# Some 32x128 products of a cross network's matmul stream split into four on 32x32 tiles

## The chip, the cores and the metric

The kernel runs on one core of one Trainium2 chip. The metric is the device time of one execution in microseconds (us). Before the change it is 467.46 us, the median of two runs (467.14 to 467.78). The span of a profile is the time from the first to the last instruction of one profiled execution.

## The reference

A cross network of six layers on a batch of 16384 rows with 416 columns, all in bf16:

```python
x = x0
for l in range(6):
    proj = jnp.einsum('bd,de->be', x, ws[l]) + bs[l]
    x = x0 * proj + x
```

`x0` is 16384 x 416, `ws` is 6 x 416 x 416, `bs` is 6 x 416.

## The kernel before

**Tiling.** The batch is cut into 8 groups `g` of 2048 rows. The activations lie transposed: features on the partitions, batch rows along the free axis. A layer's 416 features are three full tiles of 128 (`t` or `i` = 0, 1, 2) and a tail of 32. A group and a layer together are a job `(g, l)`. A job's output tile `i` has four chunks `j` of 512 batch rows, and one chunk fills one of the 8 banks of PSUM. The four tails of a group, 32 features each, share one tensor of 128 partitions, one quarter for each chunk; `quad` says which quarter a chunk has.

**A chunk's products.** The sum over 416 features is cut into 13 products of 32 features. Each is a matmul with 32 rows of the array (one row group `r` = 0 to 3) and 128 columns. The profile writes it 32\*128: 32 x 128 weights, 32 x 512 moving values, into 128 partitions of one bank. Twelve come from the full tiles (line 1040: three for each row group), the thirteenth from the tail (line 1044). Products of the four row groups can run beside each other in the array; those of one row group follow each other. At any time the four row groups work on different chunks, in different banks, and a chunk passes from one row group to the next.

**Other shapes.** The tail outputs are computed in `tails` as 128x32 tiles (line 697: 128 features into 32 partitions, four column groups beside each other), with corners of 32x32 tiles (line 685). At the beginning and the end of the kernel there are also full 128x128 matmuls (line 650), column quarters (line 638) and row and column quarters (line 665, in `rows32`, when `small` is set).

**After the products.** ScalarE reads a finished bank and adds the bias (line 550, in `evacuate_chunk`). VectorE multiplies two chunks at a time by `x0` (line 562) and adds `x` (line 567). The result is the next layer's input. With that reading the bank is free again.

**What sets the order.** Most of the kernel is one call of `stream`. Its order is written out by hand: the string `ORDER` gives for each step the row group and the chunk, with a `|` where a batch of tails stands. `replay` turns it into a list of single products with planned times (in its own units, a product takes `SLOT` = 20), sorts them by time, and hands out banks. `stream` walks that list (`plan`) and records each product in order; an entry with `r < 0` is a batch of tails. There are 6504 such products. TensorE executes in the order in which they are recorded. `Program` adds semaphore waits where an operation needs another engine's result, or a bank that another row group has written: two products on TensorE in the same row group need no wait, those of different row groups in the same bank do (the argument `row`).

The few lines that matter for the tile of a product are these:

```python
kw = dict(start=count[c] == 1, stop=count[c] == 4 * NT + 1, tile_position=(r * T32, 0))
```

## Time and profile before

| | |
|---|---|
| median of the runs | 467.46 us |
| span of the profiled execution | 465.7 us |
| mean granted TensorE clock | 0.997 |
| matmuls recorded / weight loads recorded | 7827 / 7833 |
| stream: first L1040 to the last | 40.7 to 429.1 us |
| L697 (tails, 128x32) | 33.6 us busy, x564 |
| L685 (corners, 32x32) | 7.1 us busy, x188 |
| L665 (quarters, 32x32) | 0.9 us busy, x32 |

PE is TensorE's matmuls, PEld its weight loads, DVE VectorE, ACT ScalarE, SP the queue that issues most DMAs. Each matmul has its own weight load ahead of it. Busy time is the time in which at least one instruction of the group is open, so matmuls that overlap are counted once; the mean duration of a matmul is its latency. L1040 is line 1040 of the kernel before. In the time-ordered view a line is a merged group: start in us, length in us, engine, line, operation, operands, count.

### The profile page before, as it was taken

How to read it: one execution, taken by the hardware profiler on the slowest of the kernel's cores; microseconds unless marked ns; L12 is line 12 of the kernel's file. 1: busy time of each engine (PE TensorE's matmuls, PEld its weight loads, DVE VectorE, ACT ScalarE, POOL GpSimd, SP SyncE). 2: the span in 40 equal slices, each digit the busy share in tenths (PEclk: the TensorE clock that was granted, in tenths of full speed). 3: DMA queues.
4: the chain of work that ended last, by engine and by line, in shares of the span. 5: the costliest groups of instructions: out<-in, count | busy, mean ns of one | idle time of the engine just before them, and what ended most of it. 6: DMA issues, size and time to landing. Idle time of an engine off the chain costs nothing.

```text
span 465.7 us, 17469 instructions
## 1 busy us (share of the span) xinstructions
PE 458.9 (99%) x7827; PEld 263.8 (57%) x7833; DVE 404.2 (87%) x700; ACT 379.1 (81%) x608; POOL 6.8 (1%) x15
## 2 busy tenths in 40 slices
PE   9999999999999999999999999999999999999995
PEld 5444566555556677555655556565575566755442
DVE  2887998989989899979989898888989889898897
ACT  4687888788888888888878888788887887889785
POOL 1000000000000000000000000000000000000000
PEclk9999999999999999999999999999999999999998
DMA  8986949101002978084858437990100095027899
GB/s 229 185 177 144 160 113 190 29 3 26 1 4 38 158 210 155 22 141 149 149 92 154 145 78 141 160 296 23 25 2 4 25 148 172 14 49 169 183 161 292
DMA packets 139087, 53.77 MB, mean 115 GB/s; under 512 B 112762, under 2 KB 138500, under 8 KB 139012
## 3 DMA queue, kind: packets, MB, share of 16 engines
q1 hardware_dynamic: 138856, 52.54, 52.5%
q8 instruction: 61, 1.00, 0.9%
q10 hardware_dynamic: 156, 0.11, 0.1%
q14 instruction: 14, 0.11, 0.1%
HBM read 5.97 MB, written 13.63 MB: 42 GB/s over the span
## 4 chain that ended last, share of the span: by engine, by line
PE 93%; DVE 4%; DMA 1%; issue 1%; ACT 0%; SPq 0%; DVEq 0%
PE ps L1040 70%; PE ps L697 7%; PE ps L1044 6%; PE ps L650 6%; PE ps L638 2%; PE ps L685 1%; DMA wm<-in_ws_dram 1%; DVE x L1194 1%; DVE x L1188 1%; DVE x L528 1%; DVE tw L523 1%; PE ps L671 1%; ACT tw L514 0%; PE ps L789 0%; SPq L734 0%
## 5 line engine op out<-in xcount | busy, mean ns | idle before, releaser
L1040 PE MATMUL ps<-x,wm 32*128 32x512 bf16 x6000 | 356.0, 374 | 0.0
L550 ACT ACTIVATE tw<-ps,bias 128x512 bf16<-128x512 f32 x500 | 310.5, 688 | 46.4 <-PE ps L1040 35.9
L1040 PEld LDWEIGHTS ps<-x,wm 32*128 32x128 bf16 x6000 | 212.5, 92 | 127.7 <-ACT tw L550 4.1
L562 DVE TENSOR_TENSOR tw<-tw,x 128x1024 bf16<-128x1024 bf16 x250 | 168.2, 689 | 39.6 <-ACT tw L550 38.9
L567 DVE TENSOR_TENSOR x<-tw,x 128x1024 bf16<-128x1024 bf16 x250 | 163.5, 690 | 0.3
L1044 PE MATMUL ps<-x,w 32*128 32x512 bf16 x504 | 151.7, 374 | 0.0
L1044 PEld LDWEIGHTS ps<-x,w 32*128 32x128 bf16 x504 | 42.7, 92 | 6.6
L514 ACT ACTIVATE tw<-ps,bias 128x512 bf16<-128x512 f32 (+1 forms) x46 | 35.0, 839 | 12.0 <-PE ps L671 7.9
L650 PE MATMUL ps<-x,wm 128*128 128x512 bf16 x146 | 33.6, 379 | 1.0 <-issue 0.8
L697 PE MATMUL ps<-x,wm 128*32 128x512 bf16 x564 | 33.6, 380 | 0.0
L608 ACT ACTIVATE ts<-ps,bias 128x512 bf16<-128x512 f32 x33 | 21.0, 687 | 14.7 <-PE ps L685 14.7
L523 DVE TENSOR_TENSOR tw<-tw,x 128x1024 bf16<-128x1024 bf16 (+1 forms) x35 | 21.4, 627 | 4.9 <-ACT tw L514 4.7
L650 PEld LDWEIGHTS ps<-x,wm 128*128 128x128 bf16 x152 | 13.9, 98 | 19.0 <-issue 3.2
L697 PEld LDWEIGHTS ps<-x,wm 128*32 128x32 bf16 x564 | 13.5, 96 | 18.7 <-ACT tw L550 4.7
L528 DVE TENSOR_TENSOR x<-tw,x 128x1024 bf16<-128x1024 bf16 (+1 forms) x35 | 20.6, 624 | 0.0
L612 DVE TENSOR_TENSOR x<-ts,x 128x512 bf16<-128x512 bf16 x47 | 18.4, 420 | 0.4
L610 DVE TENSOR_TENSOR ts<-ts,x 128x512 bf16<-128x512 bf16 x33 | 13.0, 418 | 0.0
L604 DVE SCALAR_TENSOR_TENSOR ts<-ps,bias,x 128x512 bf16<-128x512 f32 x14 | 10.5, 748 | 2.2 <-PE ps L685 2.2
L909 POOL COPY ost<-ot 128x512 bf16<-128x512 bf16 x6 | 5.3, 890 | 411.3 <-DMA ot<-x 411.3
L1130 PE MATMUL ps<-wm,x 128*128 128x416 bf16 x48 | 9.8, 340 | 0.1
L1182 ACT ACTIVATE x<-ps 128x416 bf16<-128x416 f32 x16 | 7.6, 518 | 2.4 <-PE ps L1130 2.4
L799 DVE COPY x<-ps 128x512 bf16<-128x512 bf16 x5 | 2.0, 423 | 8.5 <-PE ps L789 8.5
(50 smaller groups left out, 76.9 us busy)
## 6 DMA issues: line engine op xcount, KB each, us to landing
out_dram<-ost SPq DMA_DIRECT2D x6, 1664.0 KB, 7.1
x<-x SPq DMA_DIRECT2D x24, 96.0 KB, 2.3
x<-in_x_dram SPq DMA_DIRECT2D x8, 208.0 KB, 4.4
x<-in_x_dram SPq DMA_DIRECT2D x4, 416.0 KB, 8.0
out_dram<-ost SPq DMA_DIRECT2D x2, 832.0 KB, 6.0
wm<-in_ws_dram SPq DMA_DIRECT2D x5, 312.0 KB, 3.4
x<-x SPq DMA_DIRECT2D x22, 64.0 KB, 2.0
out_dram<-x SPq DMA_DIRECT2D x3, 416.0 KB, 4.8
```

Source lines behind the costliest of these rows:

```text
L514: add("act", lambda h, a=a, w=w, b0=b0: h.activation(tw[r][:, a * CH:(a + w) * CH], psum[:, b0 * CH:(b0 + w) * CH], ACT_F.Identity, bias=b ...
L523: add("dve", lambda h, a=a, e=e: h.tensor_tensor(tw[r][:, a * CH:e * CH], tw[r][:, a * CH:e * CH], x0s[s0][:, i * GC + a * CH:i * GC + e * ...
L528: add("dve", lambda h, a=a, e=e: h.tensor_tensor(xs[so][:, i * GC + a * CH:i * GC + e * CH], tw[r][:, a * CH:e * CH], src(i, a, e), ALU.ad ...
L550: add("act", lambda h: h.activation(tw[r][:, j * CH:(j + 1) * CH], bank(b), ACT_F.Identity, bias=bias[:, i, l:l + 1], scale=1.0), reads=[( ...
L562: add("dve", lambda h: h.tensor_tensor(tw[r][:, o], tw[r][:, o], x0s[s0][:, c], ALU.mult), reads=[("tw", r, k) for k in both] + [x0_tok(s0 ...
L567: add("dve", lambda h: h.tensor_tensor(xs[so][:, c], tw[r][:, o], src(i, a, a + 2), ALU.add), reads=[("tw", r, k) for k in both] + [stok(i ...
L608: add("act", lambda h: h.activation(ts[r][:, :], bank(b), ACT_F.Identity, bias=bias[:, 3, l:l + 1], scale=1.0), reads=[("ps", b), "bias"], ...
L612: add("dve", lambda h: h.tensor_tensor(x3s[so][:, :], ts[r][:, :], res, ALU.add), reads=[("ts", r)] + rtok, writes=[("x3", so), ("x3", so, ...
L650: add("pe", lambda h, t=t, j=j, k=k, w=w: h.matmul(bank(banks[j])[:, k * w:(k + 1) * w], wm[l][:, t, ecols], src(t, j, j + 1)[:, k * w:(k ...
L697: add("pe", lambda h, t=t, j=j, src=src, l=l, b=b, ro=ro, qo=qo: h.matmul(psum[qo, b * CH:(b + 1) * CH], wm[l][:, t, NT * P:D], src(t, j, ...
L1040: add("pe", lambda h, l=l, t=t, j=j, b=b, q=q, ecols=ecols, src=src, kw=kw: h.matmul(bank(b), wm[l][q, t, ecols], src(t, j, j + 1)[q, :], ...
L1044: add("pe", lambda h, l=l, b=b, q=q, ecols=ecols, s3=s3, kw=kw: h.matmul(bank(b), w3[l][q, ecols], s3[q, :], **kw), reads=tok3 + [("w3", l ...
```

## The change

Four stretches of the stream are picked by the number of tails batches that came before in the stream (`at_run`) and the product's place since the last batch (`in_run`, counted from 0). A picked product of 32 rows by 128 columns is issued as four of 32 rows by 32 columns, with the same moving values, into the four quarters of the same bank:

```diff
+        quarters = [0, 0]
         for _, r, c, b in plan:
             if r < 0:
                 ...
                 tails(due.pop(0)[1], corners_last=True, banks=c)
+                quarters[:] = [quarters[0] + 1, 0]
                 continue
             ...
+            at_run, in_run = quarters[0], quarters[1]
+            quarters[1] += 1
+            if {3: 100 <= in_run < 164, 5: 100 <= in_run < 164 and in_run % 8 == 0,
+                    7: 100 <= in_run < 164 and r == 0, 9: 100 <= in_run < 116}.get(at_run, False):
+                for m in range(4):
+                    o = slice(m * T32, (m + 1) * T32)
+                    km = dict(kw, tile_position=(r * T32, m * T32))
+                    wcols = slice(i * P + m * T32, i * P + (m + 1) * T32)
+                    if t < (NT if c < len(chunks) - keep else part):
+                        lhs, rhs, got = wm[l][q, t, wcols], src(t, j, j + 1)[q, :], [stok(t, j), wm_tok(l, i)]
+                    else:
+                        lhs, rhs, got = w3[l][q, wcols], s3[q, :], tok3 + [("w3", l, r)]
+                    add("pe", lambda h, b=b, o=o, lhs=lhs, rhs=rhs, km=km: h.matmul(
+                        psum[o, b * CH:(b + 1) * CH], lhs, rhs, **km),
+                        reads=got, writes=[("ps", b)], row=r)
+                if count[c] == 4 * NT + 1:
+                    evacuate_chunk(g, l, i, j, b, read[c])
+                continue
```

In the stream as built this picks 64 products one after another, 8 single ones (each eighth, all of row group 3), 16 single ones (row group 0's, each fourth) and 16 one after another. They are the stream's products 1189 to 1252, 2117 to 2173, 3050 to 3110 and 3880 to 3895. In the profile before they begin at 112.9, 168.1, 223.9 and 273.8 us. Every other instruction is as before. In the changed file the lines after the insertion are 20 further down: line 1040 becomes 1060, line 1044 becomes 1064, and the quarters are recorded at line 1053.

## The prediction

> **What bounds the kernel now.** I read the page from the top: busy shares, the 40 slices, the chain of waits; then the costliest groups, the time-ordered view around every change of tile shape, and the starts of single matmul records, which the trace keeps to the nanosecond (the view rounds to 10 ns).

> ```profile
> PE 458.9 (99%) x7827; PEld 263.8 (57%) x7833; DVE 404.2 (87%) x700; ACT 379.1 (81%) x608; POOL 6.8 (1%) x15
> PEclk9999999999999999999999999999999999999998
> PE 93%; DVE 4%; DMA 1%; issue 1%; ACT 0%; SPq 0%; DVEq 0%
> L1040 PE MATMUL ps<-x,wm 32*128 32x512 bf16 x6000 | 356.0, 374 | 0.0
> L550 ACT ACTIVATE tw<-ps,bias 128x512 bf16<-128x512 f32 x500 | 310.5, 688 | 46.4 <-PE ps L1040 35.9
> ```

> TensorE carries 93% of the chain and is never idle ahead of the stream's products (0.0 idle at L1040). ScalarE waits for TensorE (35.9 us), not the other way. So what TensorE loses inside the stream moves the end one for one. What it could absorb is small: only at 203.96 us does it lose more than 0.1 us to ScalarE or VectorE in the stretch concerned (the four row groups restart 68 to 260 ns late, mean 0.20 us).

> A product's 374 ns is its latency, not its pace. In the first stretch that the change touches:

> ```profile
> 114.64 0.37 PE L1044 MATMUL ps<-x,w 32*128 32x512 bf16 x1
> 114.80 0.42 PE L1040 MATMUL ps<-x,wm 32*128 32x512 bf16 x4
> 115.02 0.38 PE L1044 MATMUL ps<-x,w 32*128 32x512 bf16 x2
> 115.04 0.57 PE L1040 MATMUL ps<-x,wm 32*128 32x512 bf16 x4
> 115.26 0.37 PE L1044 MATMUL ps<-x,w 32*128 32x512 bf16 x1
> 115.28 0.56 PE L1040 MATMUL ps<-x,wm 32*128 32x512 bf16 x4
> 115.50 0.37 PE L1044 MATMUL ps<-x,w 32*128 32x512 bf16 x1
> ```

> From 114.64 to 115.50 there are 1+4+2+4+1+4 = 16 products in 0.864 us: each row group starts one every 216 ns, four groups beside each other, so 54 ns a product. A reader should take this round of 216 ns as the unit.

> Now the changes of tile shape that the kernel already makes:

> ```profile
> 85.86 0.60 PE L697 MATMUL ps<-x,wm 128*32 128x512 bf16 x8
> 86.40 0.42 PE L685 MATMUL ps<-x,w 32*32 32x512 bf16 x12
> 86.75 0.82 PE L1040 MATMUL ps<-x,wm 32*128 32x512 bf16 x10
> ```

> The last L697 starts 309 ns before the first L685; the last L685 starts 317 ns before the first L1040. In place of 216 ns a shape change costs a start-to-start of 304 to 318 ns everywhere in the stream. The way back from 32x32 to 32x128 is shown 14 times, always 317 or 318 ns after the last corner product of all. The first L1040 is always of row group 0, while that group's own last corner began up to 10 ns before the last of all (at 57.62 us, 327 ns before; at 86.75, 317). So the array waits for everything in flight, not for the one row group. A round that follows a change takes 226 to 230 ns, then 216 again.

> **The change, part by part.** It takes 104 products (64, 8, 16, 16) out of 6504 and makes 416 of 32x32 of them: 312 matmuls and 312 weight loads more. Order, banks and waits are the same: the built program has the same 1156 waits of TensorE on its own semaphore and 586 on ScalarE's, 26 of the splits carry one as before, and only a product's last quarter signals. No DMA moves, and no queue but TensorE's.

> The quarters themselves cost nothing. The kernel already has their very pattern, four column tiles of one row group, then of the next:

> ```profile
> 27.09 0.43 PE L665 MATMUL ps<-x,w 32*32 32x512 bf16 x16
> 27.31 0.42 PE L685 MATMUL ps<-x,w 32*32 32x512 bf16 x8
> ```

> Sixteen start within 50 ns (3.4 ns apart, weight loads between them), and the next set starts 227 ns after the first, a round after a change. Four products whole take 216 ns, the same four as 16 quarters 216. What costs is entering and leaving: I take entry as 309 ns from the last whole product to the first quarter (not shown for 32x128 to 32x32; the rows run from 304 to 317, and 309 is what both other ways into 32x32 take), 10 ns for the four quarters to start, 317 ns back.

> *64 in a row* (from 112.861 us). Last whole product 112.692, so the first quarter is at 113.001. One round of 227 and fourteen of 216 follow; the last round's last quarter starts 51 ns into it (16 x 3.4), at 116.300; whole products resume at 116.617 and 3 ns apart. The trace had them at 116.315, .317, .336, .363: late by 302, 303, 288, 264, mean 289, and 11 more for the next round of 227. **0.30 us.**

> *16 in a row* (from 273.829). Last whole 273.661, first quarter 273.970, 227 + 2 x 216 + 51 + 317 later 274.997, against 274.693 and on: mean 291 + 11. **0.30 us.**

> *8 alone*, each eighth product (168.091 to 171.113), all of row group 3. Last whole product 167.999, split at 168.308: late by 217. From a split on: whole products of four groups at 327 to 337, three more at 554 to 560, next split at 560 + 309 = 869. The trace has a split every 432. So 7 x 437 = 3059. After the last: four restarts late by 314, 314, 210, 121, mean 240, plus 11. **3.53 us.**

> *16 of row group 0*, each fourth (223.854 to 227.091). Entry 223.804 + 309: late by 259. From a split on: the other three groups at 327, 330, 334, next split at 334 + 309 = 643. The trace has 216. So 15 x 427 = 6405. After the last: 324, 166, 168, 121 late, mean 195, plus 11. **6.87 us.**

> Sum: 0.30 + 3.53 + 6.87 + 0.30 = **11.0 us**. Nearly all is the 24 lone splits, each two drains in which three row groups stand still. Span 465.7 + 11.0 = 476.7; the median of the runs shown lies 1.8 above the span (467.46), so 478.5.

> Bounds: entry at 304 or 317 moves 26 entries by -0.1 or +0.2. After a drain the groups start level and not staggered as planned; a bank handed from one group to another can then bind, as it does after the tails (at 219.53 us a group waits 47 ns for TensorE's own signal): 0 to 26 x 47 ns = 1.2. In the lone stretches the distances are longer than the 480 ns that such hand-overs take at 219.53, so I take 0. Absorbed at 203.96: at most 0.2, and I take 0, since that wait follows TensorE's own products. Below zero nothing reaches: no work and no wait goes. ScalarE and VectorE get later work at a lower pace; their 81% and 87% leave the end alone. Own range 477.8 to 480.1.

> **Rivals.**

> *The drain holds only the row group whose shape changes.* Then the 16 of group 0 change once in and once out (all of group 0's products in that stretch are split), the two runs likewise, 93 + 101 = 0.2 us each; only the 8 alone pay 16 times about 97 ns on group 3, with group 0 close behind it: 1.55. Sum 2.15, time 469.6: within 2%, not slower. For it: overlapping row groups, and no row with this entry. Against it: the 317 ns counted from the last of all groups, 14 times. It decides if a lone split costs under about 365 ns in the mean in place of 425 (24 x 365 + 0.6 = 9.35 us, 2%).

> *The quarters cannot be fed at that pace for long.* The burst row shows 24 tiles; the longest steady pace shown is 54 ns a pair of weight load and matmul, where 13.5 would be needed. If 54 were the limit past the first 24, the run of 64 would take 232 x 54 + 82 = 12.6 us in place of 3.45 and that of 16 2.2 in place of 0.86: 10.6 more, 489.1; half way, 483.8. The lone splits need 7 pairs in 643 ns and are not touched. Instruction loading speaks against the worst:

> ```profile
> q8 instruction: 61, 1.00, 0.9%
> ```

> 1.00 MB for 15,660 matmuls and loads is 64 bytes each, 16 KB or 256 instructions a packet, 0.9% of 16 engines' span over 61 packets is 1.1 us each; 256 quarters and loads last 1.73 us.

> [...]

> *The clock falls* where TensorE runs at a third of its pace (about 14 us): if the granted 1.00 halved there, up to 10 us more, 489. All slices show 9 but the last, the sparse first microseconds too.

> That the change does not do what it says is excluded by the built program's 416 quarters.

> **How the numbers follow.** Forecast 0.74 (478.5; 477.8 to 480.1); fed too slowly 0.13 (480 to 489); drain by row group, or an entry that does not drain, 0.09 (468 to 472); clock 0.02; something between 0.02. The range 477.2 to 484.0 holds the forecast and the lower half of the second case, about 0.79. The measurement tells 2% from no change: 476.8 is the mark. Slower by over 2%: 0.74 + 0.13 + 0.02, less 0.03 for a forecast that comes out a little under the mark, 0.86; within 2% 0.13; faster 0.01.

> **What would show it.** In the changed profile: quarters in rounds of 216 ns in the run of 64, and whole products resuming some 0.29 us late; lone splits 643 ns apart in the stretch of group 0 and 869 ns apart in that of the eight; 0.31 us from the last whole product to a quarter. If the split of group 0 follows group 3 within some 10 ns, the entry does not drain. If the run of 64 lasts over 3.8 us, the feed binds. TensorE's busy time hardly tells, since overlapping records count as busy. Wrong altogether would be a time under 476.8.

## The result and the profile after

The changed kernel takes 485.39 us (median of two runs, 485.23 to 485.56) against 467.46: 1.0383 times as long, 95% interval 1.0353 to 1.0414. The span of the profiled execution went from 465.7 to 483.7 us, 18.0 more. The prediction was 478.5 with a range up to 484.0. The direction was right, and the size 6.9 us short.

The page of the changed kernel, with the lines that answer to those shown of before (line 1040 is now 1060; the quarters are at 1053):

```profile
PE 476.3 (98%) x8139; PEld 261.6 (54%) x8145; DVE 404.4 (84%) x700; ACT 379.7 (79%) x608; POOL 6.2 (1%) x15
...
PEclk9999999999999999999679999999999999999999
...
PE 94%; DVE 3%; DMA 1%; issue 1%; ACT 0%; SPq 0%; DVEq 0%
...
L550 ACT ACTIVATE tw<-ps,bias 128x512 bf16<-128x512 f32 x500 | 311.4, 688 | 64.2 <-PE ps L1060 47.7
L1060 PE MATMUL ps<-x,wm 32*128 32x512 bf16 x5904 | 360.5, 377 | 0.0
...
L1053 PE MATMUL ps<-x,wm 32*32 32x512 bf16 x384 | 16.3, 399 | 0.0
...
L1053 PEld LDWEIGHTS ps<-x,wm 32*32 32x32 bf16 x384 | 6.1, 88 | 9.4 <-issue 6.9
```

TensorE still carries the chain (94%), and ScalarE waits for it 12 us longer in all than before (47.7 against 35.9). The clock row has a 6 and a 7 in the middle, where before had 9. And of the 9.4 us that the weight-load side stood idle ahead of the quarters' loads, 6.9 were ended by nothing that the profile shows ("issue").

Each stretch's cost is read from the starts of the stream's products, compared one by one with the trace of before (the mean of four products ahead of the stretch and of four behind it, once the delay has settled):

| stretch | predicted | measured |
|---|---|---|
| 64 in a row | 0.30 | 1.78 |
| 8 alone | 3.53 | 3.5 |
| 16 of row group 0 | 6.87 | 12.98 |
| 16 in a row | 0.30 | 0.39 |
| sum | 11.0 | 18.7 |

The 18.7 reach the last matmuls whole; the stores at the end came 0.7 us sooner behind the last VectorE operation than before, which leaves the span 18.0 longer. Two of the four stretches are as predicted to 0.1 us. The other two hold the miss, and each shows why in its own view.

**The clock.** Stretch by stretch (window in us; its length, then the busy time and the instructions of PE, PEld, DVE, ACT and POOL, then the granted clock, the DMA share and GB/s):

```profile
226.00:229.40 3.40, 3.40 (x66) 1.88 (x58) 3.40 (x9) 2.38 (x5) 0.00 (x0) 1.00 0.21 53
229.50:234.00 4.50, 4.50 (x53) 1.32 (x51) 1.64 (x3) 2.33 (x4) 0.00 (x0) 1.00 0.91 199
234.10:243.10 9.00, 9.00 (x60) 1.70 (x56) 3.35 (x6) 1.76 (x4) 0.00 (x0) 0.50 0.88 158
243.20:247.70 4.50, 4.50 (x48) 1.91 (x48) 0.69 (x1) 1.61 (x3) 0.00 (x0) 0.50 0.10 29
247.80:251.00 3.20, 3.20 (x64) 1.70 (x60) 1.86 (x4) 2.58 (x5) 0.00 (x0) 1.00 0.02 5
```

The lone splits of row group 0 begin at 229.46. For 4.6 us they run at full clock, then the clock is 0.50 from 234.05 to 247.71, some 4.5 us beyond the end of the last split. TensorE counts as busy all the time (9.00 of 9.00 us in the third window): the records overlap. The time-ordered view shows what it really does, first at full clock:

```profile
230.10 0.40 PE L1053 MATMUL ps<-x,wm 32*32 32x512 bf16 x4
230.43 0.39 PE L1060 MATMUL ps<-x,wm 32*128 32x512 bf16 x3
230.75 0.39 PE L1053 MATMUL ps<-x,wm 32*32 32x512 bf16 x4
```

and then at half:

```profile
237.24 0.61 PE L1053 MATMUL ps<-x,wm 32*32 32x512 bf16 x4
237.78 0.61 PE L1060 MATMUL ps<-x,wm 32*128 32x512 bf16 x3
238.32 0.61 PE L1053 MATMUL ps<-x,wm 32*32 32x512 bf16 x4
```

Splits are 648 ns apart (643 predicted), later about 1080.

**The gap in the run of 64.** The weight loads of the run, in order of time (in brackets the idle time ahead):

```profile
115.14 0.15 PEld L1053 LDWEIGHTS ps<-x,w 32*32 32x32 bf16 x4
116.61 0.10 PEld L1053 LDWEIGHTS ps<-x,w 32*32 32x32 bf16 x4 [1.32 <-issue]
116.62 0.15 PEld L1053 LDWEIGHTS ps<-x,wm 32*32 32x32 bf16 x16
```

From the last start before the gap to the first after it are 1.38 us; 3773 recorded instructions of TensorE lie ahead of it. Without it the run costs 0.40. A packet of 16 KB on the instruction queue (q8 on the page) had begun at 114.17 and ended at 115.05.

### The profile page after: what moved, and what is told of

It is laid out like the page before. It is cut to its first block, busy times and chain, and to the rows that moved or that the text cites. A ratio compares the mean times of both kernels' runs of the same rounds, so it can differ in the third digit from the quotient of the medians.

```text
span 483.7 us, 18093 instructions
## 1 busy us (share of the span) xinstructions
PE 476.3 (98%) x8139; PEld 261.6 (54%) x8145; DVE 404.4 (84%) x700; ACT 379.7 (79%) x608; POOL 6.2 (1%) x15
## 4 chain that ended last, share of the span: by engine, by line
PE 94%; DVE 3%; DMA 1%; issue 1%; ACT 0%; SPq 0%; DVEq 0%
PE ps L1060 68%; PE ps L697 7%; PE ps L1064 6%; PE ps L650 6%; PE ps L1053 3%; PE ps L638 2%; PE ps L685 1%; DMA wm<-in_ws_dram 1%; DVE x L1214 1%; DVE x L1208 1%; DVE x L528 1%; DVE tw L523 1%; PE ps L671 1%; ACT tw L514 0%; PE ps L789 0%
## 5 line engine op out<-in xcount | busy, mean ns | idle before, releaser
L550 ACT ACTIVATE tw<-ps,bias 128x512 bf16<-128x512 f32 x500 | 311.4, 688 | 64.2 <-PE ps L1060 47.7
L1060 PE MATMUL ps<-x,wm 32*128 32x512 bf16 x5904 | 360.5, 377 | 0.0
L1060 PEld LDWEIGHTS ps<-x,wm 32*128 32x128 bf16 x5904 | 204.7, 92 | 136.4 <-issue 10.8
L562 DVE TENSOR_TENSOR tw<-tw,x 128x1024 bf16<-128x1024 bf16 x250 | 168.1, 688 | 58.0 <-ACT tw L550 57.1
L697 PE MATMUL ps<-x,wm 128*32 128x512 bf16 x564 | 33.6, 380 | 0.0
L697 PEld LDWEIGHTS ps<-x,wm 128*32 128x32 bf16 x564 | 13.5, 96 | 18.7 <-ACT tw L550 4.7
L1053 PE MATMUL ps<-x,wm 32*32 32x512 bf16 x384 | 16.3, 399 | 0.0
L1053 PEld LDWEIGHTS ps<-x,wm 32*32 32x32 bf16 x384 | 6.1, 88 | 9.4 <-issue 6.9
```

Of the source, the lines that this page charges most:

```text
L550: add("act", lambda h: h.activation(tw[r][:, j * CH:(j + 1) * CH], bank(b), ACT_F.Identity, bias=bias[:, i, l:l + 1], scale=1.0), reads=[( ...
L562: add("dve", lambda h: h.tensor_tensor(tw[r][:, o], tw[r][:, o], x0s[s0][:, c], ALU.mult), reads=[("tw", r, k) for k in both] + [x0_tok(s0 ...
L697: add("pe", lambda h, t=t, j=j, src=src, l=l, b=b, ro=ro, qo=qo: h.matmul(psum[qo, b * CH:(b + 1) * CH], wm[l][:, t, NT * P:D], src(t, j, ...
L1053: add("pe", lambda h, b=b, o=o, lhs=lhs, rhs=rhs, km=km: h.matmul(psum[o, b * CH:(b + 1) * CH], lhs, rhs, **km), reads=got, writes=[("ps", ...
L1060: add("pe", lambda h, l=l, t=t, j=j, b=b, q=q, ecols=ecols, src=src, kw=kw: h.matmul(bank(b), wm[l][q, t, ecols], src(t, j, j + 1)[q, :], ...
```

## The experiments

All but one change only which products are split, and that one the width of the tiles; the computation stays whole. The costs below are those of the stretches, from the product starts of one trace each, as above. Times are given where they carry the verdict, and those are medians of four runs or more; the other kernels ran once.

**Without the stretch of row group 0.**

```diff
-            if {3: 100 <= in_run < 164, 5: 100 <= in_run < 164 and in_run % 8 == 0,
-                    7: 100 <= in_run < 164 and r == 0, 9: 100 <= in_run < 116}.get(at_run, False):
+            if {3: 100 <= in_run < 164, 5: 100 <= in_run < 164 and in_run % 8 == 0, 9: 100 <= in_run < 116}.get(at_run, False):
```

> The change without the stretch of row group 0 (64 in a row, 8 alone and 16 in a row stay). Theory (that stretch costs 12.9 us of the 18.0 because the granted clock halves there; the others cost what the changed trace shows, 1.75 + 3.5 + 0.4): 5.7 us over the kernel before, about 473.2, granted clock 1.00 from 230 to 260 us. Rival (the costs of the stretches hang together, for instance the clock falls because of all quarters so far): the clock still falls somewhere and the kernel stays over 475.

Measured: 473.56 us, 1.0122 times the kernel before (1.0107 to 1.0137), and 5.70 us by the starts (1.79, 3.5, 0.39). The granted clock is 1.00 up to 468.9 us, near the end. The three other stretches alone did not make the clock fall, and without the stretch of row group 0 the change would count as no change by 2%.

**The stretch of row group 0 alone.**

```diff
+            if {7: 100 <= in_run < 164 and r == 0}.get(at_run, False):
```

> Only the stretch of row group 0: 16 lone splits, each fourth product. Theory (the thin stretch alone makes the clock fall): 12.9 us over the kernel before, about 480.4; lone splits 648 ns apart at first, then some 1083 ns once the granted clock is 0.5, and the clock back about 5 us after the last split. Rival (earlier quarters are needed for the fall): 16 x 0.43 = 6.9 us, 474.4, clock 1.00 throughout.

Measured: 479.67 us (four runs, 478.55 to 480.37), 1.0257 times (1.0240 to 1.0275); in the profiled run, the quickest of the four, 11.5 us by the starts. The windows of that run:

```profile
223.90:230.00 6.10, 6.10 (x69) 1.85 (x67) 3.24 (x7) 2.68 (x5) 0.00 (x0) 1.00 1.05 163
230.10:236.20 6.10, 6.10 (x46) 1.24 (x42) 1.87 (x3) 1.19 (x2) 0.00 (x0) 0.50 1.03 205
236.30:240.20 3.90, 3.90 (x40) 1.57 (x40) 0.69 (x1) 1.97 (x3) 0.00 (x0) 0.50 0.18 50
240.30:250.00 9.70, 9.70 (x181) 4.99 (x173) 6.65 (x11) 7.50 (x13) 0.00 (x0) 1.00 0.02 3
```

The thin stretch alone made the clock fall. It fell 6.1 us after the first split in place of 4.6 and lasted 10.24 us in place of 13.65. Both lengths are whole multiples of 3.413 us (3 and 4). So are the times at full clock that the clock records of the traces show from the first record to a fall, or from a return to a fall: 228.69 and 235.52 us in the changed kernel (67 and 69), 457.39 in the kernel before (134). I read this as a clock that is set in windows of 3.413 us; since the fall came 4.6 us after the first split there and 6.1 here, they do not start with the work. As an estimate, one window at half clock loses half of 3.41, 1.7 us, and the four runs spread by 1.8. The two quicker have a mean granted clock of 0.988, the two slower one of 0.984 and 0.985, which is about a window of 3.41 us more at half: the stretch costs a window more or less by where it falls.

**Seven of its splits.**

```diff
+            if {7: 100 <= in_run < 128 and r == 0}.get(at_run, False):
```

> Only the first 7 of the 16 lone splits of row group 0, a thin stretch of 7 x 0.65 = 4.5 us. Theory (the clock falls only after a thin stretch of some 4.6 us or more, the time it took in the changed kernel): no fall, 0.22 + 6 x 0.43 + 0.2 = 3.0 us over the kernel before. If a fall needs less than 4.5 us of it, or comes later than its cause, the clock is 0.5 for some 5 us behind the stretch and the cost is about 5.5.

Measured: 3.19 us, granted clock 1.00 in the stretch and behind it. The thin stretch was 4.3 us long and filled no 3.41 us window whole (counted back from the clock's change at the kernel's end, the windows' edges lay at 225.9 and 229.3; it ran from 224.3 to 228.6). It also prices a lone split at full clock: the sixteen would have cost 3.19 + 9 x 0.432 = 7.1, so about 5.9 of the 12.98 us are the clock's.

**Two runs of 32 for the run of 64.**

```diff
+            if {3: 100 <= in_run < 132 or 228 <= in_run < 260}.get(at_run, False):
```

> The 64 in a row alone, cut into two runs of 32 with 96 whole products between. Theory (the 1.4 us stall in the run of 64 is instruction loading: TensorE asks for 256 instructions when it begins the last 256 that it has, and they come about 3.5 us later, while 32 split products use up 256 in 1.7 us): neither run of 32 empties what is loaded, so no stall, 2 x 0.40 = 0.8 us over the kernel before. Rival (the array or its sequencer falls behind after some 40 split products and must catch up): two runs of 32 lose the same 1.4 us or more in all, 1.8 to 2.2.

Measured: 0.82 us and no gap. The same 64 products, with two shape changes more, cost 0.96 us less.

**A run of 128.**

```diff
+            if {3: 100 <= in_run < 228}.get(at_run, False):
```

> Only the run of whole splits at the first place, 128 products long in place of 64 (1024 instructions). Theory (instruction loading, 3.5 us for each 256): the run meets three edges of 256 instructions, the first stall 1.4 us, the next two about 1.75 each, so 0.4 + 4.9 = 5.3 us over the kernel before, and the stalls stand exactly 256 instructions apart. Rival (a single disturbance at 115 us, such as a transfer in the way): one stall, 1.8 us.

Measured: 5.61 us with three gaps. The weight loads around them:

```profile
116.81 0.10 PEld L1052 LDWEIGHTS ps<-x,w 32*32 32x32 bf16 x4 [1.69 <-issue]
...
120.26 1.39 PEld L1052 LDWEIGHTS ps<-x,wm 32*32 32x32 bf16 x100 [1.73 <-issue]
...
123.72 0.14 PEld L1052 LDWEIGHTS ps<-x,wm 32*32 32x32 bf16 x16 [1.72 <-issue]
```

Ahead of the gaps lie 3777, 4033 and 4289 recorded instructions, so they stand exactly 256 apart, and they end 3.45 us apart. The instruction packets in the trace begin 1.11 us after each restart (117.92 after 116.81, 121.37 after 120.26) and end 0.93 and 0.97 us later; work resumes 1.4 us after that (120.26, 123.72). So from one restart to the next one packet of 16 KB, 256 instructions, arrives, and that takes 3.45 us. That each is asked for at the restart is inferred from these times; that one is under way at a time fits these times and the traces of before and of the changed kernel: the next packet begins 2.5 us or more behind the end of the last. The first gap was longer than expected, 1.75 us from start to start in place of 1.4: its packet took 1.34 us (from 113.97) where the changed kernel's took 0.88. The rival's single disturbance is out.

**Halves in place of quarters.**

```diff
+            if {3: 100 <= in_run < 164}.get(at_run, False):
-                for m in range(4):
-                    o = slice(m * T32, (m + 1) * T32)
-                    km = dict(kw, tile_position=(r * T32, m * T32))
+                for m in range(2):
+                    o = slice(m * 2 * T32, (m + 1) * 2 * T32)
+                    km = dict(kw, tile_position=(r * T32, m * 2 * T32))
...
```

> Only the 64 in a row, but each product in two of 32 rows by 64 columns in place of four by 32. Theory (instruction loading): 256 instructions last 3.45 us, nearly the 3.5 that loading takes, so no stall or one under 0.2 us; the two shape changes stay; 0.3 to 0.5 us over the kernel before. Rival (column tiles as such cannot be kept going): a stall of the same kind, over 1 us.

Measured: 0.35 us, no gap. Tiles 64 columns wide kept the full pace here: the whole cost is no more than that of two shape changes (0.39 in the run of 16). Like each run of 32, this run is 256 instructions long and no more, so it does not tell what a longer one would do.

**Four split, four whole, in turn.**

```diff
+            if {7: 100 <= in_run < 228 and in_run % 8 < 4}.get(at_run, False):
```

> At the place of row group 0: of each eight products the first four are split and the next four whole, 128 products, so 32 shape changes over some 11 us, one in each 0.34 us, as often as in the changed kernel's thin stretch, but with 8 products in 687 ns in place of 4 in 648. Theory (the clock falls because too little work goes through the array): no fall, 16 x (687 - 432) = 4.1 us over the kernel before. Rival (the shape changes themselves, or their drains, make it fall): clock 0.5 from about 4.6 us on, and 10 us or more.

Measured: 4.21 us, 692 ns for each eight products, granted clock 1.00 throughout. 32 shape changes in 11 us did not make the clock fall.

**24 lone splits, each eighth.**

```diff
+            if {5: 100 <= in_run < 292 and in_run % 8 == 0}.get(at_run, False):
```

> At the place of the 8 alone: 24 lone splits, each eighth product, a stretch of about 21 us with 8 products in some 864 ns. Theory (that much work keeps the clock, however long it lasts): no fall, 0.2 + 23 x 0.432 + 0.2 = 10.4 us over the kernel before. Rival (the eight alone were merely too short, 7 us, for the fall to come): clock 0.5 in the later part, over 15 us.

Measured: 10.46 us, splits 863 to 865 ns apart, granted clock 1.00 for the whole 20 us. So the eight alone were not merely too short to make it fall.

**Lone splits, each fifth.**

```diff
+            if {7: 100 <= in_run < 220 and in_run % 5 == 0}.get(at_run, False):
```

> At the place of row group 0: 24 lone splits, each fifth product, so that one round of four whole products stands between two splits: 5 products in some 650 ns in place of 4, with the same two shape changes in the same time. It looks for where the clock begins to fall: kept at 8 products in 864 ns (9.3 a us) and lost at 4 in 648 (6.2 a us), this has 7.7 a us. If the clock holds: 0.2 + 23 x 0.38 + 0.2 = 9.2 us over the kernel before. If it falls after 4.6 us or more: about 17 to 19.

Measured: 9.21 us, splits 652 ns apart. The window of the whole stretch:

```profile
223.60:239.00 15.40, 15.40 (x196) 4.68 (x195) 6.00 (x10) 6.39 (x10) 0.00 (x0) 1.00 0.85 155
```

The clock held for 15 us at the very period, and with the very shape changes, of the stretch that lost it. The differences are one whole product a period, and that the split's row group changes from one split to the next. The row group is no rival: each eighth product is always of row group 3, and there the clock held too.

**Row groups 0 and 1 split, 2 and 3 whole.**

```diff
+            if {7: 100 <= in_run < 164 and r < 2}.get(at_run, False):
```

> At the place of row group 0: the products of row groups 0 and 1 are split, 32 in pairs, those of 2 and 3 stay whole: still two shape changes in each four products and four products in some 650 ns. Theory (the clock goes by the work in a given time, and lone or paired is the same to it): it falls as with row group 0 alone, for three or four windows of 3.41 us, 11 to 13 us over the kernel before. Rival (what thins the array is that a lone split uses one row group): no fall, 7.1 us.

Measured: 14.4 us; the theory was right about the fall and low on its length. The clock was 0.50 from 227.15 to 244.21, five windows:

```profile
224.00:227.10 3.10, 3.10 (x52) 1.02 (x50) 0.60 (x1) 1.46 (x3) 0.00 (x0) 1.00 0.89 81
227.20:238.90 11.70, 11.70 (x114) 2.37 (x116) 4.58 (x7) 3.01 (x5) 0.00 (x0) 0.50 0.90 180
```

Here it fell 3.15 us after the first split: a window had begun 0.26 us before the stretch, and was thin nearly from end to end.

**104 splits in runs.**

```diff
+            if {3: 100 <= in_run < 132 or 228 <= in_run < 260, 5: 100 <= in_run < 108, 7: 100 <= in_run < 116, 9: 100 <= in_run < 116}.get(at_run, False):
```

> The same number of splits, 104, near the same four places, but in runs: 32 and 32 at the first, 8 in a row at the second, 16 and 16 at the third and fourth. Theory (what counts is the number of shape changes, the instruction edges met and the clock, not the number of quarters): 10 changes, no stall, no fall: 5 x 0.4 = 2.0 us over the kernel before, within 2%. Rival (the quarters cost by their number): between 10 and 18 us.

Measured: 468.75 us, 1.0024 times the kernel before (1.0014 to 1.0033); 1.97 us by the starts. The same number of quarters as in the changed kernel costs about a tenth of its 18.7. No version here beats the kernel before.

## Why the prediction was right and wrong

**The drains: right.** At each shape change of the four stretches no row group started anything for 304 to 318 ns at full clock. The entry from 32x128 to 32x32, of which before had no row, took 304 ns from the last whole product, and 314 where a drain had come just before (309 taken); the way back 327 from a split's first quarter, as predicted. The eight alone came out at 3.5 us against 3.53, and between a lone split and the products behind it no row group started anything, so the rival by row group is out. Beside a round of 216 each change lost some 90 to 100 ns.

**The runs: right in kind, 0.1 us short each.** Quarters start 3.4 ns apart in the first two rounds; from the third on mostly 8 to 9 ns apart, with single steps of up to 34, so that in the run of 16 the last quarter starts 155 ns into its round and not 51, and whole products resume 0.1 us later. The rounds ahead of the gap still follow each other every 216 ns, and a mean of 13.5 ns is all that this needs: the pace that I feared as a rival does not bind.

**The 64 in a row: the step that failed is the packet's price.** The prediction set a packet's 1.1 us against the 1.73 us that 256 quarters and loads last, and took that to speak against a feed that binds. The packet's own time was the wrong term: by the run of 128 a packet costs 3.45 us from one restart to the next. Whole products use up 256 instructions in 6.9 us (128 x 54 ns), so the trace of before could show no such gap. The gap was 1.38 us in the run of 64. The two runs of 32, and the halves, take it away. The measured time lies in the range that the prediction gave to a feed that is too slow (480 to 489), but that is luck: the feed holds 1.4 of the 7.7 us by which the sum fell short.

**The 16 of row group 0: the step that failed is the clock's chance.** The mechanism was listed and priced at up to 10 us, with a chance of 0.02, on the ground that the clock row shows 9 also in the sparse first microseconds. That ground was misread. These are the matmuls on a constant that only keep TensorE busy at the start of the kernel before, and the later ones of the same shape:

```profile
L771 PE MATMUL ps<-const-bfloat16-1.0 128*128 128x512 bf16 x7 | 3.3, 623 | 0.8 <-PEq L1264 0.8
L650 PE MATMUL ps<-x,wm 128*128 128x512 bf16 x146 | 33.6, 379 | 1.0 <-issue 0.8
```

Those of line 771 start 427 ns apart from 1.15 us on, those of line 650 215 from 6.13 us on: the first microseconds ran at half the pace. I take that for half clock, by the changed kernel: where its granted clock is 0.50, a product is recorded with 0.61 us in place of 0.39, here with 623 ns in place of 379. The row does not show it: the trace's record of the clock begins only at 5.82 us, and the row has 9 also before that. Measured, the fall cost about 5.9 us. Without it the four stretches would have cost some 12.8, about 480 us in all: still slower by over 2%, and inside the stated range. (The thin stretch was also put at about 14 us; its own sixteen times 643 ns are 10.3.)

What goes with the fall is the number of products that go through the array in a given time, as these stretches tell:

| stretch | products in a period | a us | clock |
|---|---|---|---|
| stream, all whole | 4 in 216 ns | 18.5 | 1.00 |
| four on four | 8 in 692 ns | 11.6 | 1.00 |
| each eighth | 8 in 864 ns | 9.3 | 1.00 |
| each fifth | 5 in 652 ns | 7.7 | 1.00 |
| row group 0, each fourth | 4 in 648 ns | 6.2 | falls |
| pairs | 4 in 658 ns | 6.1 | falls |

By the table the clock fell at 6.2 products a us and held at 7.7, 33% and 41% of the full pace. The windows themselves give it closer. Counted from the changes of clock, the windows that hold only products of the stream and were followed by half clock have 12 to 24 products in them, a split counted once (the three at whose end the clock fell 20, 20 and 21; in the changed kernel 21, 12, 12 and 20 in order). Those followed by full clock have 25 or more: 25, 26 and 25 in the stretch of each fifth, 27 in the first thin window of row group 0 alone, 32 where the clock came back. A window at full pace has 63, so in these runs the two kinds part at some 40% of it, at the fall and at the return alike. The number of matmuls does not part them: the window before the fall of the pairs had 50 of them, windows of each fifth 40, and those before the return 32. Whether the hardware counts products, rows in use or something else that goes with them was not separated. Nor was a thin stretch without any split tried. In all three falls, the clock fell at the end of a window that was thin for at least nine tenths, and came back at the end of the first one that was dense throughout. Each time that cost at least one window more at half pace behind the stretch.

No long pause came before the fall: in the stretch of row group 0 starts lay no more than 318 ns apart while the clock was full, and the profile shows no idle time of TensorE there.

## What to carry to other kernels

Count changes of tile shape, not matmuls: a lone odd-shaped product among others cost two stops of all four row groups here, 0.43 us, and a run of sixteen no more than a lone one, 0.39. Where the pace of products falls to a third, look at the granted clock: in the three kernels that had 16 such periods in a row it fell to 0.50, for 10.24 to 17.06 us, in the changed kernel until some 4.5 us beyond the end of the last split. And see how long TensorE takes to use up 256 instructions: the runs of 64 and 128 needed 256 in 1.73 us, and in the run of 128 they came 3.45 us apart, so loading them set the pace.

## What the runs showed of the hardware

The instruction queue moved 61 packets of 16,384 bytes in the kernel before and 63 in the changed one, for 15,660 and 16,284 recorded matmuls and weight loads: some 256 to a packet. In both traces no two packets overlap. In the run of 128 it is 1.11 us from a restart until a packet begins, 0.93 and 0.97 for the packet, and 1.4 until work resumes. The profile calls this wait "issue" (1.69 to 1.73 us of idle time ahead of the weight loads there).
